# V spread over the partitions by TensorE, a smaller first load of constants, one more half of gate rows on TensorE, and a re-planned order, in a one-core mLSTM and mixer kernel

## The chip, the cores and the metric

One core of one Trainium2 chip. The metric is the device time of one execution in microseconds (us); the time before is given as a median of three runs, and one further execution was profiled.

## The reference

An mLSTM attention over B = 4 batches, 8 heads, 768 steps and head size 40, then a channel mixer on its output x (4 x 768 x 320).

```python
for t in range(S):
    m_new = np.maximum(f_gate[:, :, t] + m, i_gate[:, :, t])
    f_stab = np.exp(f_gate[:, :, t] + m - m_new); i_stab = np.exp(i_gate[:, :, t] - m_new)
    C = f_stab * C + i_stab * (v_t outer k_t);  n = f_stab * n + i_stab * k_t
    y[:, :, t] = sigmoid(o_t) * (C q_t) / max(|n q_t|, 1)
h = x^T @ U @ V            # U: 768 x 32, V: 32 x 768, along the sequence
u = x + h^T
out = u + relu(u @ w_ch1) @ w_ch2      # 320 -> 1280 -> 320
```

The weights U, V, w_ch1 and w_ch2 come as float64 bits and are turned into float32 on the chip.

## The kernel before

Each batch is cut into two halves of 384 steps, each half into six chunks of 64 steps. For every half, `half` inside `attention` loads q and k (`load_qk`), k and v by token (`load_tk`) and the output gate (`load_o`), makes the chunk states (`kv`, `state`), the scores, the decay weights (`decay_exp` or `decay_scan`, `weigh`), the numerator (`pv` and `inter`) and the normalized, gated result in the tile x. `rows` multiplies x with U, `mix` spreads the result with V (`vst`) and adds x (`cols`, the tile ut), and `mlp` does the two large products (`up` with w1, `down` with w2). Each operand of the large products is split into a high and a low part (`w_high`, `w_low`, `ut_high`, `ut_low`, `relu_high`, `relu_low`).

**Order.** Nothing is issued where it stands in the text. Each step is registered with `p.op(kind, priority, engine, cost, function, reads, writes, new tiles)`, and `Plan.schedule` simulates the engines with those costs and issues the steps in the order that it finds. Priorities are shifted by `ORDER`, `ORDER0` (batch 0) and, for one instance of a kind, by `MOVED`. Tiles of a kind share a few buffers (`SLOTS`): three of kind "fd" hold rows broadcast over partitions, five of kind "x" hold x and, at the start, gate data. PSUM has three banks of kind "m2" and five of kind "ps"; the kinds "st", "at" and "m1" share those five (`SHARE`). Transfers go out on SyncE's queue ("sp"), two at the start on ScalarE's ("aq"). When TensorE would be idle in the first part of the run, `keep_busy` puts in fillers: products of the tile zeros (`warm`, records `m<-zeros` or `ps<-zeros`). `Plan.words` keeps count of TensorE's instructions and, by an assumed page of 256 instructions, delays the plan where the next page would not have arrived; `PAGE, SENT_ON, FETCH` are its constants.

**V.** `keep_v` (L668) receives V as float32 in a tile of 128 partitions by 192 (`VN`). `store_v` writes it to the DRAM tensor vsd, two `load_v` (L681) read it back, each half of 384 columns repeated four times over 32 partitions, into an "fd" tile. `v_high` (ScalarE, L684) scales it with a column of the constants, `v_low` (L687) subtracts, and the result is vst, read by `cols` and by the first `down`.

**Constants.** `load_consts` (L507) loads 256 columns of cst_in into cst: the identity (128 columns), a mask and three columns of zeros and ones, `C_MP, C_MV, C_MU`, used as scales in `rows_high` (L1058), `v_high` and `ut2_high` (L1095).

**Gate rows.** q is multiplied with a cumulated decay g, which is needed repeated over 64 partitions for each head. `early[1]` decides, by `4 * hf + 8 * b < GB_FROM`, whether TensorE makes the repeated rows in PSUM (`two_rows`, records `ps<-gst,cst`, eight products per pair of heads) or SyncE loads them from DRAM (`rows_of("g", ...)`, records `fd<-gsd`). With `GB_FROM = 8` TensorE makes them for both halves of batch 0, and the two halves of batches 1, 2 and 3 load them. `q_decay` (L926) multiplies.

Products and weight loads of TensorE all have line L411 (the helper `mm`), transfers line L414 (`send`).

Of the kernel before, what the change touches and what calls it, by code (L numbers as in the profile page):

```python
# [19 lines left out]
RANK = 32  # L20
# [27 lines left out]
FB_FROM, GB_FROM = 12, 8  # L48
# [5 lines left out]
ALT_PRI = 1679.3  # L54
# [9 lines left out]
    "sigmoid": -38.7, "cols": -41.6,  # L64
# [5 lines left out]
AHEAD, IN_FLIGHT, SEEN, FLIGHT_TO = 1600.0, 970000.0, 150.0, 70000.0  # L70
# [34 lines left out]
STAY, TO_QUARTERS, FROM_QUARTERS = -32.2, 120.0, 180.0  # L105
WORDS = {"scores": 96, "pv": 48, "logs": 24, "log_turn": 96, "g": 16, "up": 8, "down": 6, "cols": 8, "rows": 4, "gate_turn": 48, "totals": 16}
TABLE = {"gate_exp": 1, "gate_input_exp": 1, "decay_exp": 1, "sigmoid": 2}
TABLE_LOAD, TABLE_STAY = 1283.0, 763.5
MARGIN, PLAIN = 37.5, {"up", "down"}
MOVED = {  # L110
    "again": {7: -414},
    "cols": {8: 345, 15: 1025},
    "down": {3: 37, 15: 37, 24: 2, 25: 2, 26: 37, 28: 37, 34: 37, 36: 37, 38: 37, 48: 2, 49: 2, 50: 37, 54: 37, 60: 505, 61: 460,
# [4 lines left out]
    "gate_shift": {0: 105},  # L118
    "kv": {4: 20, 6: 1282, 7: -579},
    "load_decay": {0: 453, 2: -485, 3: -22},  # L120
    "load_g": {2: 73, 13: 319, 19: 42, 20: 86, 21: 62},
    "load_gates0": {0: -1168},
    "load_o": {1: 29, 2: -829, 3: 75, 4: 255, 5: -389, 6: 386, 8: 532, 11: 132},
    "load_qk": {0: -1226, 1: -1267, 2: -779, 3: -1534, 4: -1058, 5: -1000, 6: -664, 7: -558, 13: -1338, 16: 191, 22: 223,
        24: 246, 26: 69, 30: 805},
    "load_tk": {0: -705, 1: -501, 2: -190, 3: -273, 4: 94, 6: 291, 8: 323},
    "load_v": {0: -364, 1: -515},
    "load_weights": {0: 63, 10: 73, 11: 81},
    "norm": {3: 120},
    "out_norm": {2: -130, 3: -492, 9: -257},  # L130
    "pv": {7: 435, 10: 221, 24: 375, 27: -186, 28: 469},
    "q_decay": {25: 305},
    "rows": {1: 261, 2: 418, 8: 132, 13: 541, 15: 777, 17: 387, 18: 124},
    "scores": {3: -1036, 10: 444, 12: 232},
    "state": {12: -92, 14: 159, 16: 220, 27: 461},
    "state0": {7: -386},
    "store_decay": {0: -1444, 1: 276},
    "store_g": {0: -284, 1: 149},
    "store_v": {0: 229},
    "u_low": {0: -343},  # L140
    "up": {16: 36, 32: 36, 40: 424, 43: 116, 44: 424, 46: 424, 58: 424, 64: 507, 78: 215, 81: 61, 82: 61, 83: 243, 84: 243,
        96: 61, 104: 61},
    "upto": {0: 250},
    "ut_high": {8: 356, 10: -148},
    "v2": {8: -907},
    "v_high": {0: -226},
    "vi": {0: 675, 8: 376, 10: -769, 11: -122, 15: -181},
    "w13_high": {2: 909},
    "w13_low": {3: 273},
    "w_high": {5: 70},  # L150
    "w_low": {2: -269},
    "weigh": {24: 475},
    "weight_rebase": {19: 381},
    "weight_shift": {13: 486},
    "weight_tail": {5: 409, 11: -509},
    "x_low": {0: -449, 2: 247, 17: -670},
# [3 lines left out]
PAGE, SENT_ON, FETCH = 256, 64, 2900.0  # L160
# [3 lines left out]
class Plan:  # L164


    def __init__(self, slots):
        self.kind_of, self.count, self.spare = [], [], []
        self.slots = {tag: [[tile, 0.0, None, tag] for tile in tiles] for tag, tiles in slots.items()}
        self.ops, self.at, self.busy, self.port = [], {}, defaultdict(float), []  # L170
        self.writer, self.readers = {}, defaultdict(list)
        self.batch = 0
        self.fetched, self.page_at = 12, {}
        self.seen = Counter()
        self.placed_by, self.uses, self.slot, self.held = {}, Counter(), {}, Counter()
# [40 lines left out]
    def words(self, n, at, cost, dma):  # L216

        a, late = self.fetched, 0.0
        self.fetched += n
        for x in range(a, self.fetched + 1):  # L220
            if x > a and (x + SENT_ON) % PAGE == 0:
                t = at + late + cost * (x - a) / n
                page = (x + SENT_ON) // PAGE
                self.page_at[page + 1] = max(t + max(0.0, dma - t), self.page_at.get(page, 0.0)) + FETCH
            if x < self.fetched and x % PAGE == 0:
                late += max(0.0, self.page_at.get(x // PAGE, 0.0) - (at + late + cost * (x - a) / n))
        return late
# [160 lines left out]
def mlstm_mixer_kernel(  # L388
# [43 lines left out]
    cst = const.tile([P, C_HSEL], F32, name="cst")  # L432
    ident = cst[:, C_IDENT:C_IDENT + P]
# [16 lines left out]
    vsd = dram.tile([RANK, S], F32, name="vsd")  # L450
# [38 lines left out]
    def gates():  # L489
# [17 lines left out]
        p.op("load_consts", -97, "aq", dma(P * C_HSEL * 4), lambda: send(nc.scalar, out=cst, in_=cst_in[:, 0:C_HSEL]), w=[("cst",)])  # L507
# [160 lines left out]
    def keep_v(pri, kc, t):  # L668

        p.op("store_v", pri, "sp", dma(P * VN * 4), lambda: send(nc.sync, out=vsd.rearrange("r (a n) -> (r a) n", n=VN), in_=t()), r=[kc], w=[("vsd",)])  # L670
        for c in range(2):
            cs = slice(c * HS, (c + 1) * HS)
            k4, kv = ("v4", c), ("vm", c)

            def v4(k4=k4):
                return T[k4][:, 0:HS]

            def load(cs=cs, v4=v4):
                send(nc.sync, out=v4(), in_=vsd[:, cs].unsqueeze(0).to_broadcast([P // RANK, RANK, HS]))
# [56 lines left out]
    def attention(b, base):  # L736
# [10 lines left out]
        def half(hf, n):  # L747
# [40 lines left out]
            for e2 in range(2):  # L788
                p.op("v2", at(n - 1), ("pool", "dve"), (pool(VO) * 0.79, dve(VO)), lambda e, e2=e2: e.tensor_mul(  # L789
                    v2flat()[:, e2], vflat()[:, e2], tokv(1, hf)[:, e2]),  # L790
                     r=[(kt, "v", 0), (kt, "v", 1), ("tok", hf, 1)], w=[(kv2, e2)], new=[(kv2, "v2")] if e2 == 0 else [])
            for e2 in range(2):
                p.op("vi", at(n - 1), ("pool", "dve"), (pool(VO) * 0.79, dve(VO)), lambda e, e2=e2: e.tensor_mul(  # L793
                    vflat()[:, e2], vflat()[:, e2], tokv(0, hf)[:, e2]),
                     r=[("tok", hf, 0), (kt, "v", 0), (kt, "v", 1), (kv2, e2)], w=[(kt, "vi", e2)])
# [10 lines left out]
            def chunks():  # L806
                def kvmm():
                    for j in range(nk):
# [8 lines left out]
                     w=kk, new=[(k, "at") for k in kk], stream="att", load=0.85, words=32 * nk)  # L817
# [226 lines left out]
        for c in range(NC):  # L1044
# [13 lines left out]
            lambda: nc.scalar.activation(T[kr], T[kp][:, 0:DM], AF.Copy, scale=cst[:, C_MP:C_MP + 1]),  # L1058
            r=[kp, ("cst",)], w=[kr], new=[(kr, "prr")],
# [4 lines left out]
    def mix(b, hf, pri):  # L1064
# [4 lines left out]
        for c in range(3):  # L1069
# [30 lines left out]
    def mlp(b, hf, pri):  # L1100
# [32 lines left out]
        def down(m, n):  # L1133
# [16 lines left out]
            p.op("down", pri + m + LAG + 0.5, "pe", 588 if m == 0 else 441, ops, r=r, w=[ka], new=[(ka, "m2")] if m == 0 else [])  # L1150
# [134 lines left out]
```

## Time and profile before

| what | us |
|---|---|
| median of three runs | 352.3 (350.09 to 355.05) |
| the profiled execution, its own time | 350.27 |
| its span, first to last instruction | 348.5 |
| TensorE busy in the span | 333.6 |
| VectorE, ScalarE, GpSimd busy | 209.7, 120.9, 68.0 |

The times of the engines are sums of recorded spans. TensorE's busy time holds the fillers, too. A record that ends in brackets, `[1.11 <-issue]`, tells how long its engine was idle before it and what ended that; "issue" is a wait for nothing that the profile shows. PE is TensorE, DVE VectorE, ACT ScalarE, POOL GpSimd, SPq the queue of SyncE.

### The profile page before, as it was taken

What the parts mean: (1) busy time and instruction counts of PE and PEld (TensorE: products, weight loads), DVE (VectorE), ACT (ScalarE), POOL (GpSimd) and SP (SyncE); (2) the same over time, 40 slices, a digit from 0 to 9 for tenths busy, and PEclk for the clock granted to TensorE, in tenths of its full rate; (3) what the DMA queues carried; (4) which work ended last, traced back from release to release, by engine and by line L of the source; (5) the groups of instructions that cost most, each with busy time, mean ns of one, the idle gap of its engine ahead of it and who ended that gap; (6) DMA issues with size and microseconds to landing.
All of it is one profiled execution on the core that took longest, in us unless ns stands there. A gap on an engine that the chain in (4) does not pass through costs nothing.

```text
span 348.5 us, 11236 instructions
## 1 busy us (share of the span) xinstructions
PE 333.6 (96%) x4794; PEld 305.5 (88%) x4794; DVE 209.7 (60%) x457; ACT 120.9 (35%) x279; POOL 68.0 (20%) x83
## 2 busy tenths in 40 slices
PE   8987898999999999989999999899999999999996
PEld 5655665799999999989899998799999999999996
DVE  7799897878985657965873229771575133121322
ACT  5258377646732034123143124210434122011220
POOL 1232524323260101422041006260030000000000
PEclk9999998999999999999999999989999999999999
DMA  6879656779845492575574103430010000100101
GB/s 180 186 220 229 187 175 194 223 218 256 241 134 197 136 222 81 182 176 130 150 192 132 44 2 93 156 86 2 3 58 3 0 2 0 56 2 0 58 0 56
DMA packets 23002, 40.63 MB, mean 117 GB/s; under 512 B 4201, under 2 KB 15721, under 8 KB 22953
## 3 DMA queue, kind: packets, MB, share of 16 engines
q1 hardware_dynamic: 22760, 39.70, 40.8%
q8 instruction: 37, 0.61, 0.7%
q10 hardware_dynamic: 192, 0.23, 0.2%
q14 instruction: 13, 0.10, 0.1%
HBM read 35.68 MB, written 4.23 MB: 115 GB/s over the span
## 4 chain that ended last, share of the span: by engine, by line
PE 77%; DMA 10%; DVE 4%; SPq 4%; issue 4%; ACT 1%; DVEq 0%; ACTq 0%
PE ps L411 46%; PE m L411 31%; SPq L414 4%; DMA kv<-in_tk 4%; DMA fd<-gsd 2%; DMA raw<-in_w 2%; DMA qk<-in_qk 2%; DVE dm L935 1%; DVE qd L926 1%; DVE cv L649 1%; DVE cv L651 0%; DVE x L1015 0%; DVE kv L793 0%; DVE wt L943 0%; ACT h L1049 0%
## 5 line engine op out<-in xcount | busy, mean ns | idle before, releaser
L411 PE MATMUL m<-w2h,h 128*128 128x320 f32 x480 | 119.6, 314 | 0.0
L411 PE MATMUL ps<-ut,w1h 128*128 128x384 f32 x400 | 117.3, 343 | 0.5 <-DVE wt L943 0.2
L1130 DVE SCALAR_TENSOR_TENSOR h<-ps,h 128x384 fp32r<-128x384 f32 x80 | 43.1, 553 | 77.0 <-ACT h L1128 69.2
L411 PEld LDWEIGHTS m<-w2h,h 128*128 128x128 f32 x480 | 83.4, 188 | 1.3 <-DVE h L1130 0.3
L1128 ACT ACTIVATE h<-ps 128x384 fp32r<-128x384 f32 x80 | 38.4, 490 | 126.6 <-PE m L411 86.3
L411 PE MATMUL ps<-ut,w1l 128*128 128x384 f32 x240 | 81.2, 338 | 0.0
L411 PEld LDWEIGHTS ps<-ut,w1h 128*128 128x128 f32 x400 | 74.4, 190 | 2.2 <-DVE wt L943 0.5
L411 PE MATMUL m<-w2l,h 128*128 128x320 f32 x240 | 74.3, 310 | 0.0
L411 PEld LDWEIGHTS ps<-ut,w1l 128*128 128x128 f32 x240 | 45.6, 190 | 0.0
L411 PEld LDWEIGHTS m<-w2l,h 128*128 128x128 f32 x240 | 45.3, 189 | 0.1
L1010 POOL TENSOR_TENSOR og<-og,rd 128x480 f32<-128x480 f32 x13 | 13.4, 1037 | 64.1 <-DVE rd L1005 57.9
L935 DVE TENSOR_TENSOR_SCAN dm<-fd,ident 128x384 f32<-128x384 f32 x20 | 21.2, 1070 | 3.9 <-DMA fd<-fsd 3.9
L411 PE MATMUL ps<-qk 40*64 40x64 f32 x768 | 17.3, 223 | 4.5 <-issue 3.0
L411 PEld LDWEIGHTS ps<-qk 40*64 40x64 f32 x768 | 14.6, 134 | 7.7 <-issue 4.7
L1153 DVE TENSOR_TENSOR o<-m,x 128x320 f32<-128x320 f32 x24 | 11.0, 486 | 14.5 <-PE m L411 14.4
L943 DVE TENSOR_TENSOR wt<-ps,dm 128x384 f32<-128x384 f32 x32 | 16.3, 548 | 4.8 <-PE ps L411 4.8
L411 PEld LDWEIGHTS <-zeros 128*128 128x128 bf16 (+1 forms) x114 | 10.7, 104 | 7.8 <-issue 4.9
L789 POOL TENSOR_TENSOR v<-kv,tok 128x492 f32<-128x492 f32 x7 | 9.0, 1292 | 37.3 <-PE ps L411 27.2
L411 PE MATMUL m<-zeros 128*128 128x256 bf16 x104 | 15.5, 287 | 0.1
L411 PE MATMUL ps<-cst,x 128*128 128x128 f32 (+2 forms) x168 | 15.1, 237 | 0.0
L926 DVE TENSOR_TENSOR qd<-qk,fd 104x320 f32<-104x320 f32 (+1 forms) x18 | 9.3, 519 | 9.0 <-DMA fd<-gsd 8.6
L830 POOL TENSOR_TENSOR Ct<-C,dect 104x164 f32<-104x164 f32 x16 | 9.3, 582 | 27.3 <-DVE C L831 27.1
(113 smaller groups left out, 410.4 us busy)
## 6 DMA issues: line engine op xcount, KB each, us to landing
kv<-in_tk SPq DMA_DIRECT2D x16, 486.0 KB
qk<-in_qk SPq DMA_DIRECT2D x64, 120.0 KB
raw<-in_w SPq DMA_DIRECT2D x20, 320.0 KB
og<-in_tk SPq DMA_DIRECT2D x16, 240.0 KB
fd<-fsd SPq DMA_DIRECT2D x40, 96.0 KB
out<-o SPq DMA_DIRECT2D x24, 160.0 KB
fd<-gsd SPq DMA_DIRECT2D x24, 96.0 KB
fd<-gsd SPq DMA_DIRECT2D x24, 80.0 KB
```

Of the source, the lines that this page charges most:

```text
L411: nc.tensor.matmul(o, a, b, start=start, stop=stop, **kw)
L414: p.sent = queue.dma_start(**kw).ins
L649: p.op("weight_shift", pri, "dve", 69 + n / 1.92, lambda tu=tu: V.tensor_scalar(tu(), tu(), 3, None, ALU.logical_shift_left), w=[kc], port ...
L789: p.op("v2", at(n - 1), ("pool", "dve"), (pool(VO) * 0.79, dve(VO)), lambda e, e2=e2: e.tensor_mul(v2flat()[:, e2], vflat()[:, e2], tokv(1 ...
L830: e.tensor_mul(t, cview(hf, j - 1)[r], dect[r, hf, b, :, j:j + 1].to_broadcast([Q + D, NP, DV]))
L926: e.tensor_mul(T[kqd][:, tg], T[kqk][:, 0, tg], T[kgb][0:Q + D, tg])
L935: lambda: nc.vector.tensor_tensor_scan(T[kdm], T[kfb][:, 0:HS], ident6, 0.0, ALU.mult, ALU.add),
L943: p.op("weigh", at(u), "dve", dve(HS), lambda: nc.vector.tensor_mul(T[kw], T[ks][:, 0:HS], T[kdm]), r=[ks, kdm], w=[kw], new=[(kw, "wt")])
L1010: p.op("out_norm", pf, ("pool", "dve"), (pool(KO) * 0.79, 900), lambda e, m=m, rdv=rdv: e.tensor_mul(otv(m), otv(m), rdv().unsqueeze(3).to ...
L1128: p.op("relu_high", pri + m - 1000, "act", 371, lambda: nc.scalar.activation(T[kh][:, 0, :], T[kp][:, 0:HS], AF.Relu), r=[kp], w=[(kh, 0)] ...
L1130: p.op("relu_low", pri + m - 1000, "dve", dve(HS), lambda: nc.vector.scalar_tensor_tensor(T[kh][:, 1, :], T[kp][:, 0:HS], 0.0, f32(T[kh][: ...
L1153: p.op("residual", pri - 1000, "dve", dve(DM), lambda: nc.vector.tensor_add(T[ko], T[ka][:, 0:DM], T[X][:, n, 0:DM]), r=[ka] + [(X, m) for ...
```

## The change

V is no longer sent through DRAM. ScalarE builds a selection matrix out of the identity (`v_pick`, 512 elements), in a tile of kind "x", and four products of 192 columns (`v_rows`, two for each half) write the repeated V into PSUM tiles of kind "st"; `v_high` and `v_low` read it there, and `v_low` is VectorE's alone. The first load of constants is cut to the identity (128 columns), and a small transfer on SyncE, `load_cols`, brings the columns of scales. `GB_FROM` goes from 8 to 12: the first half of batch 1 gets its gate rows from TensorE. The plan's page model, its constants and its counts of instructions are changed, and so are the priorities. `v2` and `vi` are only written differently.

```diff
-FB_FROM, GB_FROM = 12, 8
+FB_FROM, GB_FROM = 12, 12
-ALT_PRI = 1679.3
+ALT_PRI = 1765.5
-    "sigmoid": -38.7, "cols": -41.6,
+    "sigmoid": -38.7, "cols": -120.0,
-AHEAD, IN_FLIGHT, SEEN, FLIGHT_TO = 1600.0, 970000.0, 150.0, 70000.0
+AHEAD, IN_FLIGHT, SEEN, FLIGHT_TO = 1500.0, 1070000.0, 150.0, 70000.0
-STAY, TO_QUARTERS, FROM_QUARTERS = -32.2, 120.0, 180.0
+STAY, TO_QUARTERS, FROM_QUARTERS = -197.1, 120.0, 180.0
-TABLE_LOAD, TABLE_STAY = 1283.0, 763.5
-MARGIN, PLAIN = 37.5, {"up", "down"}
+TABLE_LOAD, TABLE_STAY = 1283.0, 1078.0
+MARGIN, PLAIN = 0.0, {"up", "down"}
 MOVED = {
...
-PAGE, SENT_ON, FETCH = 256, 64, 2900.0
+PAGE, SENT_ON, FETCH = 256, 64, 2750.0
...
-        self.fetched, self.page_at = 12, {}
+        self.fetched, self.page_at = 18, {}
...
-        for x in range(a, self.fetched + 1):
-            if x > a and (x + SENT_ON) % PAGE == 0:
-                t = at + late + cost * (x - a) / n
-                page = (x + SENT_ON) // PAGE
-                self.page_at[page + 1] = max(t + max(0.0, dma - t), self.page_at.get(page, 0.0)) + FETCH
-            if x < self.fetched and x % PAGE == 0:
-                late += max(0.0, self.page_at.get(x // PAGE, 0.0) - (at + late + cost * (x - a) / n))
+        for x in range(a, self.fetched):
+            if (x + SENT_ON) % PAGE == 0:
+                page, t = (x + SENT_ON) // PAGE, at + late + cost * (x - a) / n
+                wait = max(0.0, self.page_at.get(page, 0.0) - t)
+                late, t = late + wait, t + wait
+                self.page_at[page + 1] = max(t, dma, self.page_at.get(page, 0.0)) + FETCH
...
-    cst = const.tile([P, C_HSEL], F32, name="cst")
-    ident = cst[:, C_IDENT:C_IDENT + P]
+    ident = const.tile([P, P], F32, name="ident")
+    groups = const.tile([P, 3], F32, name="groups")
...
-        p.op("load_consts", -97, "aq", dma(P * C_HSEL * 4), lambda: send(nc.scalar, out=cst, in_=cst_in[:, 0:C_HSEL]), w=[("cst",)])
+        p.op("load_consts", -97, "aq", dma(P * P * 4), lambda: send(nc.scalar, out=ident, in_=cst_in[:, 0:P]), w=[("cst",)])
+        p.op("load_cols", 0, "sp", dma(P * 12 * 4), lambda: send(nc.sync, out=groups, in_=cst_in[:, C_MP:C_MU + 1]), w=[("cols",)])
...
     def keep_v(pri, kc, t):
-        p.op("store_v", pri, "sp", dma(P * VN * 4), lambda: send(nc.sync, out=vsd.rearrange("r (a n) -> (r a) n", n=VN), in_=t()), r=[kc], w=[("vsd",)])
+        kpick, reps = ("pick",), P // RANK
+        def pick():
+            return T[kpick].rearrange("p c d -> p (c d)")[:, 0:reps * P].rearrange("p (a x) -> p a x", x=P)
+        p.op("v_pick", pri - 1, "act", 50 + act(reps * P), lambda: nc.scalar.copy(
+            pick().rearrange("p a (n r) -> p a n r", n=reps),
+            ident.rearrange("p (r a) -> p a r", a=reps).unsqueeze(2).to_broadcast([P, reps, reps, RANK])), r=[("cst",)], w=[kpick], new=[(kpick, "x")])
         for c in range(2):
...
-            p.op("load_v", pri, "sp", dma(P * HS * 4), load, r=[("vsd",)], w=[k4], new=[(k4, "fd")], stream="v", load=0)
+            def spread(kp=kp, c=c):
+                for n in range(2):
+                    mm(T[kp][:, n * VN:(n + 1) * VN], pick()[:, 2 * c + n], t(), skip_group_check=True)
+            p.op("v_rows", pri, "pe", 2 * 4 * VN / 2.4 + 60, spread, r=[kc, kpick], w=[kp], new=[(kp, "st")], stream="mix", words=8)
...
-            p.op("v_low", pri, *both(HS), lambda e, kv=kv, v4=v4, cs=cs: e.tensor_sub(
-                vst[:, cs], v4(), f32(T[kv])), r=[k4, kv], w=[("vst", c)])
+            p.op("v_low", pri, "dve", dve(HS), lambda kv=kv, kp=kp, cs=cs: nc.vector.tensor_sub(
+                vst[:, cs], T[kp][:, 0:HS], f32(T[kv])), r=[kp, kv], w=[("vst", c)])
```

## Rows read from the trace of the kernel before

**Rows 1.** The page: TensorE's busy time, and its granted clock in 40 slices.

```profile
PE 333.6 (96%) x4794; PEld 305.5 (88%) x4794; DVE 209.7 (60%) x457; ACT 120.9 (35%) x279; POOL 68.0 (20%) x83
...
PEclk9999998999999999999999999989999999999999
```

**Rows 2.** Busy time by stretch: length, PE, PEld, DVE, ACT, POOL, clock, DMA share, GB/s.

```profile
0.00:65.00 65.00, 56.82 (x1411) 38.95 (x1411) 55.28 (x133) 39.53 (x85) 21.17 (x29) 0.97 0.72 195
65.00:130.00 65.00, 64.48 (x752) 60.63 (x753) 50.13 (x111) 27.49 (x69) 16.42 (x17) 1.00 0.73 204
130.00:240.00 110.00, 106.97 (x1752) 101.81 (x1752) 69.03 (x141) 29.11 (x73) 27.70 (x35) 0.98 0.41 115
240.00:348.50 108.50, 105.29 (x884) 104.11 (x882) 35.29 (x73) 24.74 (x54) 2.71 (x3) 1.00 0.05 19
...
28.00:65.00 37.00, 31.06 (x817) 21.83 (x810) 32.01 (x82) 26.02 (x57) 14.91 (x18) 0.95 0.68 192
```

**Rows 3.** The same for instructions on the tile zeros, the fillers (PE first).

```profile
0.00:65.00 65.00, 18.54 (x114) 10.66 (x114) 0.17 (x1) 1.25 (x1) 0.97 0.72 195
...
28.00:65.00 37.00, 7.01 (x50) 4.23 (x50) 0.00 (x0) 0.00 (x0) 0.95 0.68 192
```

**Rows 4.** PE's waits: sum, times, longest; two before 66 us, the last behind.

```profile
PE ps L411 <- issue: 2.7, 3, 1.0
PE ps L411 <- DMA qk<-in_qk: 1.1, 1, 1.1
...
PE ps L411 <- issue: 2.8, 3, 1.4
```

**Rows 5.** Timeline of PE: start, us, record; two of seven waits for issue.

```profile
29.27 0.49 PE L411 MATMUL m<-C,qd 40*64 40x41 f32 x19 [1.11 <-issue]
...
225.54 0.40 PE L411 MATMUL ps<-qk 40*64 40x64 f32 x11 [1.38 <-issue]
```

**Rows 6.** Timeline of PE: first large product in, first behind the second clock drop.

```profile
227.98 0.52 PE L411 MATMUL ps<-ut,w1h 128*128 128x384 f32 x1
...
230.71 0.33 PE L411 MATMUL ps<-ut,w1l 128*128 128x384 f32 x1
```

**Rows 7.** Timeline, 53 to 62 us: V's loads, its split, and its first reader.

```profile
53.01 1.26 SPq L414 DMA_DIRECT2D fd<-vsd  x2
...
58.75 0.62 ACT L684 ACTIVATE rru<-fd,cst 128x384 fp32r<-128x384 f32 x1 [1.17 <-DMA fd<-vsd]
...
60.38 0.62 DVE L1042 TENSOR_TENSOR pst<-ps,prr 128x320 fp32r<-128x320 f32 x2 [0.43 <-ACT prr L1058]
...
61.21 0.62 ACT L684 ACTIVATE rru<-fd,cst 128x384 fp32r<-128x384 f32 x1 [0.86 <-DMA fd<-vsd]
...
61.37 0.42 PE L411 MATMUL ps<-vst,pst 128*128 128x384 f32 x1
```

**Rows 8.** The chain that ended last, before 65 us: start, us, what.

```profile
51.50 3.23 DMA qk<-in_qk
...
54.80 7.09 DMA raw<-in_w
```

**Rows 9.** Timeline of SPq: first and last of four pairs of gate-row loads.

```profile
37.79 1.13 SPq L414 DMA_DIRECT2D fd<-gsd  x2
...
61.95 1.50 SPq L414 DMA_DIRECT2D fd<-gsd  x2
```

**Rows 10.** Timeline: the nearest rows to the added products and the added copy.

```profile
20.00 0.75 PE L411 MATMUL ps<-gst,cst 64*64 64x320 f32 x8
...
34.94 0.67 ACT L661 CAST u<-cv 128x576 fp32r<-128x576 f32 x1
...
46.06 0.81 PE L411 MATMUL ps<-x,u 128*128 128x320 f32 x2
```

**Rows 11.** Timeline of PE: a wait for the product of q and g.

```profile
64.05 0.78 PE L411 MATMUL ps<-C,qd 40*64 40x41 f32 x36 [0.68 <-DVE qd L926]
```

**Rows 12.** Timeline of ACT: the first reader of the constants.

```profile
4.01 1.03 ACT L554 COPY ident<-cst 64x384 f32<-64x384 f32 x2 [0.26 <-DMA cst<-in_cst_in]
```

More of the change, by code (lines that the diff above doesn't have):

```diff
@@ L104 @@
 QUARTERS = {"logs", "log_turn", "g", "scores", "kv", "pv", "inter", "gate_turn", "totals"}
-STAY, TO_QUARTERS, FROM_QUARTERS = -32.2, 120.0, 180.0
-WORDS = {"scores": 96, "pv": 48, "logs": 24, "log_turn": 96, "g": 16, "up": 8, "down": 6, "cols": 8, "rows": 4, "gate_turn": 48, "totals": 16}
+STAY, TO_QUARTERS, FROM_QUARTERS = -197.1, 120.0, 180.0
+WORDS = {"scores": 98, "pv": 48, "logs": 24, "log_turn": 98, "g": 16, "up": 8, "down": 6, "cols": 8, "rows": 4, "gate_turn": 48, "totals": 16}
 TABLE = {"gate_exp": 1, "gate_input_exp": 1, "decay_exp": 1, "sigmoid": 2}
-TABLE_LOAD, TABLE_STAY = 1283.0, 763.5
@@ L109 @@
-MARGIN, PLAIN = 37.5, {"up", "down"}
+TABLE_LOAD, TABLE_STAY = 1283.0, 1078.0
+MARGIN, PLAIN = 0.0, {"up", "down"}
 MOVED = {
-    "again": {7: -414},
-    "cols": {8: 345, 15: 1025},
-    "down": {3: 37, 15: 37, 24: 2, 25: 2, 26: 37, 28: 37, 34: 37, 36: 37, 38: 37, 48: 2, 49: 2, 50: 37, 54: 37, 60: 505, 61: 460,
[4 rows of a table removed]
[L118 to L156, printed above, removed]
@@ new lines @@
+    "again": {3: 561},
+    "cols": {6: 194, 8: 558, 11: -508, 15: 592},
+    "down": {4: -17, 5: -17, 7: -17, 8: -17, 15: 59, 26: 59, 28: 59, 29: -17, 32: 22, 36: 59, 49: -17, 50: 59, 54: 59, 61: 251,
[4 rows of a table added]
+    "fence": {2: -495, 3: -2310},
+    "gate": {1: -206},
+    "gate_shift": {0: 410},
+    "gate_w": {0: 1196},
+    "idents": {0: 221},
+    "inter": {6: -814, 8: -824, 11: -762},
+    "kv": {1: 795, 4: 300, 5: 342, 6: 1486},
+    "load_cols": {0: 109},
+    "load_decay": {0: 725, 1: 257, 2: 558, 26: 349, 27: 1265},
@@ new lines @@
+    "load_gates0": {0: -304},
+    "load_o": {0: 234, 1: -398, 6: 553, 8: 763},
+    "load_qk": {8: 208, 12: -173, 15: 329, 16: 505, 21: 326, 22: 389, 30: 1058},
+    "load_tk": {0: 96, 2: 192, 5: 412, 6: 658, 7: 31},
+    "load_weights": {0: 239, 1: 330, 3: -521, 4: 125, 9: 50, 10: -311, 12: -1221, 13: 251},
+    "out_norm": {7: -781},
+    "pv": {13: 676, 15: -760, 17: -864, 19: -610, 23: -252, 24: 575, 26: 834, 28: 1094},
+    "q_decay": {13: 295},
+    "residual": {15: 1582},
+    "rows": {9: 52, 15: 483, 16: 169},
@@ L157 @@
+    "rows_low2": {0: 1972},
+    "scores": {12: -404, 15: -647},
+    "spread": {0: -1577},
+    "state": {11: 234, 13: -385, 14: -406, 16: 195, 21: 422},
+    "store_decay": {0: 265, 1: 479},
+    "store_g": {0: 196, 1: 533},
[8 rows of a table added]
+    "w_high": {0: -316, 4: 140},
+    "w_low": {2: -434, 13: 157},
+    "weigh": {7: -415},
+    "weight_rebase": {5: -397, 9: -1504},
+    "weight_shift": {8: 243, 10: 543},
+    "weight_tail": {0: 338, 4: -438, 5: -509, 11: -670, 13: -215},
+    "x_high": {1: -804},
 }
@@ L668, in keep_v @@
     def keep_v(pri, kc, t):
-        p.op("store_v", pri, "sp", dma(P * VN * 4), lambda: send(nc.sync, out=vsd.rearrange("r (a n) -> (r a) n", n=VN), in_=t()), r=[kc], w=[("vsd",)])
+        kpick, reps = ("pick",), P // RANK
[4 more added lines that the diff above has]
+            ident.rearrange("p (r a) -> p a r", a=reps).unsqueeze(2).to_broadcast([P, reps, reps, RANK])), r=[("cst",)], w=[kpick], new=[(kpick, "x")])
         for c in range(2):
             cs = slice(c * HS, (c + 1) * HS)
[L673 to L679, printed above, removed]
-            p.op("load_v", pri, "sp", dma(P * HS * 4), load, r=[("vsd",)], w=[k4], new=[(k4, "fd")], stream="v", load=0)
+            kp, kv = ("v4", c), ("vm", c)
+            def spread(kp=kp, c=c):
+                for n in range(2):
+                    mm(T[kp][:, n * VN:(n + 1) * VN], pick()[:, 2 * c + n], t(), skip_group_check=True)
+            p.op("v_rows", pri, "pe", 2 * 4 * VN / 2.4 + 60, spread, r=[kc, kpick], w=[kp], new=[(kp, "st")], stream="mix", words=8)
             p.op(
                 "v_high", pri, "act", 120 + act(HS),
-                lambda kv=kv, v4=v4: nc.scalar.activation(T[kv], v4(), AF.Copy, scale=cst[:, C_MV:C_MV + 1]),
-                r=[k4, ("cst",)], w=[kv], new=[(kv, "rru")],
-            )
-            p.op("v_low", pri, *both(HS), lambda e, kv=kv, v4=v4, cs=cs: e.tensor_sub(
-                vst[:, cs], v4(), f32(T[kv])), r=[k4, kv], w=[("vst", c)])
+                lambda kv=kv, kp=kp: nc.scalar.activation(T[kv], T[kp][:, 0:HS], AF.Copy, scale=groups[:, 1:2]),
+                r=[kp, ("cols",)], w=[kv], new=[(kv, "rru")],
+            )
+            p.op("v_low", pri, "dve", dve(HS), lambda kv=kv, kp=kp, cs=cs: nc.vector.tensor_sub(
+                vst[:, cs], T[kp][:, 0:HS], f32(T[kv])), r=[kp, kv], w=[("vst", c)])
     def keep_hl(name, wh, wl, c, fs, rows):
@@ L787, in half @@
                 p.op("load_o", at(n + 4) - 8, "sp", dma(P * KO * 4), load_o, w=[(ko, m)], new=[(ko, "og")] if m == 0 else [])
[L788 to L795, printed above, removed]
+            for name, n2, dst in (("v2", 1, v2flat), ("vi", 0, vflat)):
+                for e2 in range(2):
+                    p.op(name, at(n - 1), ("pool", "dve"), (pool(VO) * 0.79, dve(VO)), lambda e, e2=e2, n2=n2, dst=dst: e.tensor_mul(
+                        dst()[:, e2], vflat()[:, e2], tokv(n2, hf)[:, e2]),
+                         r=[("tok", hf, n2), (kt, "v", 0), (kt, "v", 1)] + ([(kv2, e2)] if n2 == 0 else []),
+                         w=[(kv2, e2) if n2 else (kt, "vi", e2)], new=[(kv2, "v2")] if n2 and e2 == 0 else [])
             for m in range(2):
@@ L816, in chunks @@
                 p.op("kv", at(n - 0.5), "pe", 50 + 148 * nk, kvmm, r=[(kt, "k", 0), (kt, "k", 1), (kv2, 0), (kv2, 1)],
-                     w=kk, new=[(k, "at") for k in kk], stream="att", load=0.85, words=32 * nk)
+                     w=kk, new=[(k, "at") for k in kk], stream="att", load=0.85, words=32 * nk + 1)
                 r = slice(0, Q + D)
@@ L1057, in attention @@
             "rows_high", base + RP, "act", 50 + act(DM),
-            lambda: nc.scalar.activation(T[kr], T[kp][:, 0:DM], AF.Copy, scale=cst[:, C_MP:C_MP + 1]),
-            r=[kp, ("cst",)], w=[kr], new=[(kr, "prr")],
+            lambda: nc.scalar.activation(T[kr], T[kp][:, 0:DM], AF.Copy, scale=groups[:, 0:1]),
+            r=[kp, ("cols",)], w=[kr], new=[(kr, "prr")],
         )
@@ L1095, in mix @@
                 p.op("ut2_high", pri - 200, "act", 464, lambda kp=kp, kr=kr: nc.scalar.activation(
-                    T[kr], T[kp][:, 0:HS], AF.Copy, scale=cst[:, C_MU:C_MU + 1]), r=[kp, ("cst",)], w=[kr])
+                    T[kr], T[kp][:, 0:HS], AF.Copy, scale=groups[:, 2:3]), r=[kp, ("cols",)], w=[kr])
                 p.op("ut2_low", pri - 200, "dve", dve(HS), lambda kp=kp, kr=kr: nc.vector.tensor_sub(
@@ L1149, in down @@
                 r += [(kst, 0)] + [("vst", c) for c in range(2)]
-            p.op("down", pri + m + LAG + 0.5, "pe", 588 if m == 0 else 441, ops, r=r, w=[ka], new=[(ka, "m2")] if m == 0 else [])
+            p.op("down", pri + m + LAG + 0.5, "pe", 588 if m == 0 else 441, ops, words=8 if m == 0 else 6, r=r, w=[ka], new=[(ka, "m2")] if m == 0 else [])
             if last:
```

1 line of the change is left out of this document (removed), and 16 rows, old and new, of the table MOVED.

## The prediction

> **What bounds the kernel now.** I read the page first: TensorE is busy 333.6 of 348.5 us [rows 1], so the question is what the remaining 14.9 us are, and how much of the busy time is no work. The table by stretches cuts the run in two [rows 2]. Up to 65 us TensorE is busy 56.8 us, and the same table for the tile zeros gives 18.5 us of that to fillers [rows 3]: 38.3 us of work in 65, so 26.7 us are lost. From 65 us on it is busy 64.5 + 107.0 + 105.3 = 276.7 of 283.5 us, with no fillers. Of the 6.8 us missing there, 2.8 us are waits for "issue" [rows 4]; the stretch from 240 us lacks 3.2 us, nearly all behind the last product. So behind 65 us an engine other than TensorE hardly matters: the end comes when TensorE has worked off its list. Time can be gained in three ways: the front gets shorter (the large products start sooner, or more attention of batch 1 is done among the fillers), the waits for "issue" go, or the stretches of half clock go.
>
> What holds the front is in the chain that ended last: from 51.5 to 61.9 us it is two transfers, q and k with 3.23 us and weights with 7.09 us [rows 8], and TensorE waited 1.1 us itself for q and k [rows 4]. From 28 to 65 us the DMA share is 0.68 at 192 GB/s, and VectorE is busy 32.0 of 37 us [rows 2], so neither is quite full. The "issue" waits are seven: 2.7 us in three and one of 1.11 before 66 us, 2.8 us in three behind, 6.6 us together [rows 4, 5]. They stand inside runs of many small products (both rows shown cut one such run in two), where instructions are used up fastest; that fits instructions arriving late, but the profile names no cause. [...]
>
> **The change part by part.** The sum is made against the profiled execution: 350.27 us, its span of 348.5 and 1.8 around it. The median, 352.3, lies 2.0 above.
>
> *V.* One store and two loads go from SyncE's queue, and with them the wait of ScalarE: 1.17 and 0.86 us idle in front of the two scalings [rows 7]. V is not late for its first reader: the first half is scaled by 59.4 us, while the other operand, pst, is ready at 60.38 + 0.62 = 61.0, and the reader starts at 61.37. What goes is a detour of ScalarE right before the first large products: the second scaling occupies it until 61.8, and behind it in its queue stand a weight conversion and the copies of ut that the large products need. Bounds: 0 (the weights that arrive at 61.9 are awaited anyway) and 0.86 + 0.62 = 1.5 us. I take 0.7 gained, the middle, as the chain passes through both. Added are a copy of 512 elements on ScalarE, about 0.67 x 512/576 = 0.6 us, and four products of 192 columns: two of 320 took 0.81 us, so 0.81/2 x 192/320 = 0.24 each, 1.0 together [rows 10]. U's weights, that arrived just before V's, were split at 35 us [rows 10], so these steps can run then, when TensorE still has 7.0 us of fillers to 65 us [rows 3]; I cost them at nothing, and at +1.0 if they run where no filler is left. The four steps of the split stay and move earlier.
>
> *Gate rows of batch 1, first half.* Eight loads of 80 KB leave SyncE's queue, four pairs of 1.1 to 1.5 us between 38 and 63 us [rows 9]. TensorE gets two groups of eight products; one such group took 0.75 us [rows 10], so 1.5 us. Fillers cover it again, 2.5 of 7.0 us with V; without that cover it costs +1.5. The products with q stay.
>
> *The transfers.* 8 x 80 KB of gate rows, 96 + 2 x 192 KB of V and 64 KB of constants are 1.2 MB less, at 192 GB/s 6.3 us of traffic. That is one end; the other is 0, if what is freed was hidden. The wait of TensorE nearest to it is the 1.1 us for q and k, issued right behind two of the loads and the store that go; the weights behind them come sooner too. I take 1.5 gained, near that row, and keep 0 and 6.3 for the range.
>
> *The first constants.* Their first reader waited 0.26 us for them [rows 12]; VectorE's chain of gates, which runs beside it, did not. Bounds 0 and 0.26 gained; I take 0. The transfer added on SyncE is one issue of some 0.4 us among transfers that nobody waits for yet: 0.
>
> *The page model and the priorities.* They issue nothing, they only reorder. Bounds: all seven waits gone, 6.6 us gained, and as many again behind 65 us, 2.8 lost. Runs of small products remain and have to be fetched, so most waits should stay; I take 1.5 gained, one wait in the front and part of one behind. The half clock follows such waits: the second drop covers 2.7 us of large products [rows 6], at half speed 1.4 us lost. I take half of one such drop, 0.7 gained, with bounds of 2.8 gained (both drops) and 2.8 lost (two more). The new priorities alone I take at 0, between 2 lost and 2 gained, for no row prices them.
>
> [...]
>
> Sum: 0.7 + 1.5 + 1.5 + 0.7 = 4.4 us gained, 345.9 for an execution like the profiled one, and 2.0 more, 347.9, on the scale of the median.
>
> **The rivals.** (a) Hidden: the front is held by VectorE (busy 0.87 of it, [rows 2]) and the order of its queue, the transfers were covered, and the waits for "issue" only move. What is left is V's 0.7 us, nearly nothing else: 351.5. For it speaks that the chain runs through VectorE's queue from 62 us to the first large product; against it, that two transfers fill the ten us before.
>
> (b) The front was paced by transfers. Then most of the 6.3 us comes back, with two or three waits for "issue" and the clock drop that follows the wait at 54: 5 + 2.5 + 1.4 = 8.9 us gained, 343.4. For it: V's loads, issued at 53.0, were used at 58.75 and 61.21 and lay beside the weights' 7.09 us [rows 7, 8]. Against it: a DMA share of 0.68 [rows 2]. [...]
>
> (c) Slower: PSUM. The added g rows need two of the five shared banks at once, beside scores and decay rows of the same half, and free them only after VectorE's product with q, for which TensorE already once waited 0.68 us [rows 11]. If the two groups are pushed behind 65 us, no filler pays for them: 1.5 + 1.0 of products, two such waits of 0.7, and a new half-clock stretch of 1.4 are 5.3 lost, less 1.5 of transfers, 3.8 lost: 356.1. It decides from the point at which the groups run later than the first large product.
>
> **How the numbers follow.** What three runs can tell is about 2%, 7 us: below 345.3 or above 359.3. Forecast 0.50, (a) 0.25, (b) 0.16, (c) 0.09. The likeliest gives 347.9, its own range 345 to 350.5. To hold 8 in 10 the range takes in (a) and all but the far end of (b), and leaves out most of (c): 343.0 to 353.0. Faster by over 2%: most of (b), 0.13, and the low edge of the forecast, 0.06, so 0.19; slower by over 2%: the far part of (c), 0.04; within: 0.77.
>
> **What would show it.** V right: no transfer on vsd, four products from V's tile near 35 to 45 us, vst written before 50 us. Transfers right: TensorE's wait for q and k near 54 us gone, and the first product of ut with w1 before 63.5 us (now 64.9). Gate rows right: fillers from 28 to 65 us down to about 4 us with no more real work lost. Page model right: the sum of "issue" waits of TensorE at 4 to 5 us. The prediction is wrong if the first large product starts later than now, if "issue" waits grow, or if TensorE waits for VectorE's products with q.

## The result, and the profile after

The changed kernel takes 347.56 us (median of 20 executions, 343.89 to 352.3), the kernel before 352.65 (20, 347.65 to 357.25). The ratio is 0.9876, 95% interval [0.9843, 0.9909]: 4.4 us less, as much as the sum of the prediction, and under the 2% that count as faster. Every ratio here leaves out the executions that took over 1.5% longer than the fastest of their kernel, so this one is not the quotient of the two medians, which are 5.1 us apart. The profiled execution took 347.63 us, with a span of 345.9; against the profile of before it is 2.6 us shorter, so the pair shows somewhat less than the medians.

TensorE's busy time and its granted clock on the page of the changed kernel:

```profile
PE 332.8 (96%) x4799; PEld 307.1 (89%) x4799; DVE 208.9 (60%) x462; ACT 121.2 (35%) x280; POOL 61.5 (18%) x78
...
PEclk9989789999999999999999999999999999999999
```

The slice near 230 us that stood at 8 before [rows 1] stands at 9; the lower slices now lie in the front alone. The table by stretches, with the columns of [rows 2]:

```profile
28.00:65.00 37.00, 31.50 (x791) 22.87 (x784) 29.18 (x77) 21.34 (x49) 11.84 (x14) 0.91 0.73 197
0.00:65.00 65.00, 56.64 (x1409) 41.35 (x1410) 53.46 (x133) 36.17 (x80) 16.93 (x25) 0.92 0.73 196
65.00:130.00 65.00, 64.50 (x758) 61.38 (x757) 51.06 (x113) 30.80 (x75) 16.80 (x18) 1.00 0.64 180
130.00:240.00 110.00, 109.13 (x1774) 103.16 (x1773) 69.71 (x145) 30.62 (x76) 25.78 (x33) 1.00 0.41 117
240.00:346.00 106.00, 102.55 (x864) 101.17 (x862) 34.62 (x72) 23.56 (x51) 1.99 (x3) 1.00 0.06 20
```

From 65 us to the end there are now 280.9 us instead of 283.5; so the whole difference of the two spans lies behind 65 us. TensorE is idle there for 4.7 us (0.50 + 0.87 + 3.35) where it was 6.8, and busy 0.6 us less. Nearly all of the idle time that went is in the stretch from 130 to 240 us, which lost 3.0 us before and loses 0.9 now. The front looks the same in sum: 56.64 us busy instead of 56.82. Its inside is different. The fillers, the same table for the tile zeros:

```profile
0.00:65.00 65.00, 16.09 (x95) 0.92 0.73 196
28.00:65.00 37.00, 4.80 (x29) 0.91 0.73 197
```

So 2.45 us of fillers [rows 3] went, and their place was taken by products of V and gate rows and by a lower clock (0.92 instead of 0.97). TensorE's waits, before 66 us and then behind (sum, times, longest):

```profile
PE ps L411 <- issue: 3.4, 3, 1.7
PE m L411 <- issue: 2.2, 2, 2.0
...
PE ps L411 <- DVE x L1018: 0.7, 1, 0.7
...
PE m L411 <- DVE h L1133: 0.6, 1, 0.6
PE ps L411 <- DVE h L1133: 0.4, 1, 0.4
PE ps L411 <- issue: 0.2, 1, 0.2
```

The wait for q and k [rows 4] is gone. The waits for "issue" fell from 2.8 to 0.2 us behind 66 us and grew from 3.8 to 5.6 in the front. The chain that ended last still passes a transfer of weights in the front, 6.40 us where there were 3.23 and 7.09 [rows 8]:

```profile
52.38 3.62 PE ps L411 x62
...
58.49 6.40 DMA raw<-in_w
```

And the timeline shows the new steps, and the first large product:

```profile
3.79 1.12 ACT L675 COPY x<-ident 128x512 f32<-128x512 f32 x1
...
41.48 2.93 PE L411 MATMUL ps<-cv,x 128*128 128x192 f32 x8
...
43.78 0.56 DVE L692 TENSOR_TENSOR vst<-ps,rru 128x384 fp32r<-128x384 f32 x1
48.83 0.49 DVE L692 TENSOR_TENSOR vst<-ps,rru 128x384 fp32r<-128x384 f32 x1
53.65 0.77 PE L411 MATMUL ps<-gst,ident 64*64 64x320 f32 x8
61.78 0.77 PE L411 MATMUL ps<-gst,ident 64*64 64x320 f32 x8
66.86 0.44 PE L411 MATMUL ps<-ut,w1h 128*128 128x384 f32 x1
```

### The profile page after: what moved, and what is told of

Same layout as the page of the kernel before. It is cut to its first block, busy times and chain, and to the rows that moved or that the text cites. A ratio compares the mean times of both kernels' runs of the same rounds, so it can differ in the third digit from the quotient of the medians.

```text
span 345.9 us, 11218 instructions
## 1 busy us (share of the span) xinstructions
PE 332.8 (96%) x4799; PEld 307.1 (89%) x4799; DVE 208.9 (60%) x462; ACT 121.2 (35%) x280; POOL 61.5 (18%) x78
## 4 chain that ended last, share of the span: by engine, by line
PE 89%; DMA 4%; issue 3%; DVE 2%; SPq 0%; ACT 0%; POOL 0%; DVEq 0%; POOLq 0%; ACTq 0%
PE ps L411 52%; PE m L411 37%; DMA fd<-gsd 2%; DMA raw<-in_w 2%; SPq L414 0%; DVE x L1018 0%; DVE h L1133 0%; ACT C L825 0%; POOL qd L929 0%; DVE wt L946 0%; DVE cv L651 0%; DVE qd L929 0%; DVE o L1156 0%; DVE Ct L833 0%; DVE rd L1010 0%
## 5 line engine op out<-in xcount | busy, mean ns | idle before, releaser
L411 PEld LDWEIGHTS ps<-ut,w1h 128*128 128x128 f32 x400 | 73.4, 188 | 1.4 <-DVE ut L1100 0.3
L1013 POOL TENSOR_TENSOR og<-og,rd 128x480 f32<-128x480 f32 x12 | 12.1, 1016 | 34.5 <-DVE rd L1008 34.5
L411 PE MATMUL ps<-qk 40*64 40x64 f32 x768 | 15.8, 221 | 1.9 <-issue 1.5
L411 PEld LDWEIGHTS ps<-qk 40*64 40x64 f32 x768 | 13.7, 134 | 4.3 <-issue 2.2
L411 PE MATMUL ps<-ident,x 128*128 128x128 f32 (+2 forms) x168 | 15.2, 236 | 0.2 <-issue 0.2
L411 PEld LDWEIGHTS ps<-kv,wt 64*64 64x64 f32 x576 | 10.5, 134 | 4.9 <-issue 1.8
L833 POOL TENSOR_TENSOR Ct<-C,dect 104x164 f32<-104x164 f32 x13 | 8.2, 629 | 37.3 <-DVE C L834 25.1
L795 POOL TENSOR_TENSOR kv<-kv,tok 128x492 f32<-128x492 f32 x9 | 9.6, 1075 | 27.2 <-DVE v L795 27.1
L411 PEld LDWEIGHTS <-zeros 128*128 128x128 bf16 (+1 forms) x95 | 8.9, 106 | 6.0 <-issue 3.3
L411 PE MATMUL m<-zeros 128*128 128x256 bf16 x90 | 13.8, 290 | 0.0
```

The source lines that it names most:

```text
L411: nc.tensor.matmul(o, a, b, start=start, stop=stop, **kw)
L795: p.op(name, at(n - 1), ("pool", "dve"), (pool(VO) * 0.79, dve(VO)), lambda e, e2=e2, n2=n2, dst=dst: e.tensor_mul(dst()[:, e2], vflat()[: ...
L833: e.tensor_mul(t, cview(hf, j - 1)[r], dect[r, hf, b, :, j:j + 1].to_broadcast([Q + D, NP, DV]))
L1013: p.op("out_norm", pf, ("pool", "dve"), (pool(KO) * 0.79, 900), lambda e, m=m, rdv=rdv: e.tensor_mul(otv(m), otv(m), rdv().unsqueeze(3).to ...
```

## The experiments

Two theories stood after this reading. **L**: the gain is in the late waits for "issue", which the re-planned order avoids; V and the gate rows only change the front, where nothing came out shorter. **F**: V and the gate rows pay, because the front then leaves less work to be done behind it. "Late" waits are those behind 66 us.

To try parts without a new plan, the order that the plan had found was written into each kernel as a list, one step to a line (`kind number engine buffers`; `~` is a filler, with the number of pieces it is cut into; `>` says which transfer waits for which), and only the lines named below were changed. Line numbers in their profiles differ for that.

**e1: the changed kernel with its instructions shifted.** The first 48 fillers are cut in two. They take the same columns, and everything behind them stands 96 instructions later in TensorE's program.

```diff
-~ m2 0 1
+~ m2 0 2
...
```

> Order of the changed kernel, kept word for word; only the first 48 fillers are each cut into two halves of 128 columns, so that every later TensorE instruction stands 96 places further on against the pages of 256 instructions. Theory L (the gain is that behind 65 us no page ends inside a run of small products): TensorE's waits for issue behind 65 us go from 0.2 us to between 2 and 3.5 us, perhaps with a stretch of half clock, and the time goes back towards that of the kernel before: ratio to before 0.994 to 1.002. Theory F (the gain is V off DRAM, fewer transfers and the gate rows, in the front): ratio stays near 0.988, between 0.985 and 0.991.

Measured: 0.9906 [0.9865, 0.9947], TensorE's waits behind 66 us:

```profile
PE m L1975 <- DVE h L2697: 1.6, 1, 1.6
PE ps L1975 <- issue: 1.5, 2, 0.8
```

The waits for "issue" came back to 1.5 us, less than L wanted: where instructions stand in the program matters for them. The ratio lies in F's range, at its upper end; beside the changed kernel's 0.9876, and its 0.9893 in e8, the intervals overlap, so it is not shown that part of the gain went with them.

**e2: V and gate rows alone, in the old order.** As many records of fillers were taken out as products put in, so that the later instructions keep their numbers.

```diff
-FB_FROM, GB_FROM = 12, 8
+FB_FROM, GB_FROM = 12, 12
-load_g 0 sp fd.2
...
-load_g 7 sp 
+g 4 pe m2.1,m2.2
+g 5 pe ps.1,m2.0
-store_v 0 sp 
-load_v 0 sp fd.0
-load_v 1 sp fd.1
+load_cols 0 sp 
+v_pick 0 act x.0
+v_rows 0 pe ps.4
+v_rows 1 pe m2.1
...
```

> Order of the kernel before, kept word for word, with the two parts of the change that move work: V by four products on TensorE with the small load of constants, and the gate rows of batch 1, first half, on TensorE. Each added product takes the place of as many instructions of fillers, so that pages end where they ended. Theory L: waits for issue behind 65 us stay at 2.8 us within 0.5, ratio 0.996 to 1.003. Theory F: the whole gain or most of it, ratio 0.986 to 0.992, and the first large product at or before 63.5 us.

Measured: a median of 351.62 us (344.16 to 356.42, 6) beside 354.36 of before, too few for an interval. The profile had 3.0 us of late waits for "issue", and its first large product started at 66.17 us, not by 63.5 as F wanted. The kernel was run again as e7 and e10.

**e3: five steps moved, nothing else.** Late in the old order, five steps of large products are put into runs of small ones, so that instructions are used up more slowly there.

```diff
-down 63 pe 
...
+down 63 pe 
+up 47 pe 
...
-down 122 pe m2.0
...
+down 122 pe m2.0
+down 124 pe 
+down 125 pe 
...
```

> Kernel before, with five steps of the large products moved in the issue order and nothing else: one down step later and one up step earlier, both to stand in front of the kv step near 148 us, one down step later and two earlier, into the run of small products near 222 us. Theory L: the two long waits for issue there (1.12 and 1.38 us) and the half clock behind the second go; 2.5 to 4.2 us gained, ratio 0.988 to 0.993. Theory F: the waits are covered by other slack, ratio 0.998 to 1.002.

Measured: 0.9953 [0.9907, 0.9999], 1.7 us. Its waits behind 66 us:

```profile
PE ps L2008 <- DVE qd L2523: 1.7, 1, 1.7
PE ps L2008 <- issue: 0.6, 2, 0.4
```

2.2 us of "issue" went, and 1.7 us of the total, between the ranges of L and F. The wait of 1.7 us for q's product is the one of [rows 11], which falls behind 66 us in this execution, at 68.74. So L is right that the late waits cost time, though the interval ends just below 1, and the middle of it is less than half of the whole gain.

**e4: all three**, the edits of e2 and e3 together.

> Both edits together: V and the gate rows on TensorE in the old order, and the five moved steps. Theory L: as with the moved steps alone, within 1 us of it, ratio 0.986 to 0.994. Theory F: as with V and gate rows alone. If both parts pay, the gains add up.

Measured: 0.9822 [0.9757, 0.9888], late waits for "issue" 0.2 us. That is further than e3 (the intervals do not touch), so V and the gate rows pay something of their own, and pure L falls. What is V's and what the gate rows', the next four runs ask, on one chip.

**e5: V alone** (the V lines of e2's edit).

> V alone, everything else in the recorded order of before; the late runs of small products stay as they are, only shifted by V's 16 instructions. If the gain of the change is all in late waits for pages (theory L), the waits for issue behind 66 us stay at 2.5 to 3.2 us and the ratio is 0.997 to 1.003. If V's detour through DRAM cost what the prediction said (theory F), the ratio is 0.996 to 0.999 (0.7 us) and vst is written before 50 us without any gain behind 65 us. If the four products of V, run at half clock for 2.9 us, cost more than they free, it is 1.003 to 1.008.

Measured: 0.9972 [0.9934, 1.001]. Both theories' ranges hold this, so it doesn't part them. The late waits stayed (3.7 us), TensorE's wait for q and k is gone from the front, but the chain of the front shows what comes next when V's transfers are gone, the loads of gate rows:

```profile
43.55 4.87 DMA raw<-in_w
...
61.43 4.47 DMA fd<-gsd
```

**e6: the gate rows alone** (the lines of e2's edit with `GB_FROM`, `load_g` and `g`).

> Only the gate rows of batch 1's first half made by TensorE, in the recorded order of before; eight loads of 80 KB go, sixteen products of 0.1 us come. Theory L: ratio 0.997 to 1.003, late issue waits 2.5 to 3.2 us. Theory F (the transfers held the front): TensorE's wait for q and k near 54 us is gone and the ratio is 0.988 to 0.996 (1.5 to 4 us).

Measured: 0.993 [0.9875, 0.9985], in F's range, though the interval reaches into L's, with 3.2 us of late waits left, and the wait for q and k gone here as well. Now V's transfers are what the chain passes:

```profile
53.00 7.40 DMA fd<-vsd
```

**e7: V and gate rows again.**

> V and the gate rows together in the old order, for a ratio. Theory L: 0.997 to 1.003 with 3.0 us of late waits for issue. Theory F: 0.988 to 0.994, about the sum of the two parts, and with the five moved steps (0.9953 alone) 0.982 to 0.988, as was measured for all three. Of the executions, those at a mean granted clock of 0.995 or more should be 3 us shorter than those at 0.985, in both theories.

Measured: 0.9874 [0.9804, 0.9943], with late waits for "issue" as before the change:

```profile
PE ps L1968 <- issue: 3.3, 3, 1.6
PE ps L1968 <- DVE wt L2505: 0.2, 1, 0.2
```

Its chain passes no transfer between 41 and 70 us; VectorE's products and small products of TensorE stand there:

```profile
54.78 0.57 DVE x L2577
55.40 0.35 PE m L1968
55.99 0.87 PE ps L1968 x40
57.18 3.88 PE ps L1968 x30
61.09 0.54 ACT prr L2620
```

The gain is there with all late waits in place: F holds for these two parts together.

**e8: the changed kernel itself, beside them.**

> The changed kernel itself, on the same chip as its parts. Both theories: 0.984 to 0.991. If the order that the plan found adds something to V, the gate rows and the moved steps, it is below 0.982; if it gives back part of what they bring, it is above 0.985.

Measured: 0.9893 [0.9836, 0.995]. The late waits are 0.6 us, those of the front 7.0 (4.1 and 2.9), and the chain passes 4.11 us of weights at 50.20. So the new order adds nothing visible to V and the gate rows alone. Above 0.985 stood for an order that gives part back; the interval reaches below that, so it is not decided.

The next question was why the gate rows pay: because eight transfers of 80 KB leave the queues (**T**), or because nobody waits for what they bring, nor for their buffers (**B**).

**e9: the traffic put back.** e7 with the eight loads at their old places and with their old order among the transfers; they write a corner of w2l that is not yet in use, and nobody reads it.

```diff
+dummy_g 0 sp 
+> dummy_g 0 load_tk 5
+dummy_g 1 sp 
...
+> load_weights 13 dummy_g 7
```

> V and the gate rows on TensorE as before, but the eight loads of the gate rows stay at their places in SyncE's queue, with the order between transfers that hung on them; they write a corner of w2l that is not yet in use, and nobody reads what they bring. If the gate rows pay because eight transfers of 80 KB leave the front (theory T), 2 us of the gain go: ratio 0.992 to 0.998, and TensorE's waits in the front grow again by 1 to 2 us. If they pay because q's product no longer waits for the loads and their buffers (theory B), it stays at 0.985 to 0.990.

Measured: 0.9856 [0.9778, 0.9934]. From 28 to 65 us the transfers moved more than in e7, in the first line here e9, and no slower front followed:

```profile
28.00:65.00 37.00, 32.82 (x865) 22.27 (x857) 31.64 (x84) 26.93 (x59) 12.77 (x18) 0.93 0.71 201
```

(e7:)

```profile
28.00:65.00 37.00, 32.93 (x811) 22.18 (x805) 31.59 (x83) 27.54 (x61) 13.81 (x18) 0.93 0.63 181
```

The chain of e9 has no transfer between 41 and 70 us either. So 20 GB/s more cost nothing that can be seen, and the 2 us that T wanted are not there; a smaller price is not excluded, since the interval reaches to 0.9934. That leaves B, but no run tested B by itself, and the trace of before doesn't show its wait: VectorE was not idle before any of its four products of q with the loaded rows of this half (such records end without brackets). The last three:

```profile
56.67 0.48 DVE L926 TENSOR_TENSOR qd<-qk,fd 104x320 f32<-104x320 f32 x1
...
63.51 0.48 DVE L926 TENSOR_TENSOR qd<-qk,fd 104x320 f32<-104x320 f32 x1
...
65.94 0.48 DVE L926 TENSOR_TENSOR qd<-qk,fd 104x320 f32<-104x320 f32 x1
```

What the loads cost, through their buffers or through the transfers queued behind them, stays open.

**e10 and e11: V and gate rows, and all three, on that chip.**

> V and the gate rows without those loads, on the same chip: 0.985 to 0.990 in both theories, waits for issue behind 66 us at about 3 us.

> V, the gate rows and the five moved steps, in the old order. If the two gains add, 0.979 to 0.986, lower than V and the gate rows alone by 0.003 to 0.008, with waits for issue behind 66 us below 0.7 us; if the first such number was chance, 0.985 to 0.990.

Measured: e10 0.9932 [0.9867, 0.9997], late waits 3.9 us; e11 0.986 [0.9795, 0.9925], late waits 1.2, more than expected. Both stand higher than their first runs (e10 above its expected range, too), e11 below e10 by 0.007, as expected. In e10, the same kernel as e7, the chain does pass a transfer, of the output gate:

```profile
52.38 2.39 DMA og<-in_tk
```

All three in the old order gave 0.9822 and 0.986, the changed kernel 0.9876 and 0.9893: perhaps better by 2 us, but the intervals overlap, so no version here is shown to beat it.

**All runs at one clock.** Every execution lists its mean granted clock, and the spread of a kernel hangs on it: e2's one execution at 1.0 took 344.16 us, its four at 0.98 to 0.985 between 350.99 and 352.26. A fit over 178 executions, with a constant for each kernel (for before, one for each of the series e1 to e4, e5 to e8 and e9 to e11) and one slope, gives 1.4 us less (+- 0.2, as all errors here 95%) for each 0.005 more of mean clock, and against before at the same clock:

| | ratio as measured | us at the same clock |
|---|---|---|
| V (e5) | 0.9972 | -0.6 +- 1.3 |
| gate rows (e6) | 0.993 | -2.1 +- 1.3 |
| both (e2, e7, e10) | -, 0.9874, 0.9932 | -2.9, -2.8, -1.9 (+- 1.7 at most) |
| both, loads put back (e9) | 0.9856 | -2.5 +- 1.8 |
| five steps moved (e3) | 0.9953 | -2.5 +- 1.3 |
| all three (e4, e11) | 0.9822, 0.986 | -5.5, -5.0 (+- 1.7) |
| changed kernel (e8) | 0.9893 | -2.7 +- 1.7 |
| changed kernel shifted (e1) | 0.9906 | -1.5 +- 1.3 |

Within these errors the parts add up: 2.1 + 0.6 for both, and 2.5 more for the moved steps are 5.2. The loads put back in e9 cost 0.1 +- 1.8 us beside the mean of the three runs without them. The errors are on the small side: e1 to e4 and e5 to e8 ran on one chip, and the constants of before differ by 1.5 us between them. With one constant for that chip the rows of e1 to e4 become smaller, and those of e5 to e8 larger, by 0.7 us.

## Why the prediction came out right, point by point

**The sum.** 4.4 us were forecast and 4.4 measured. The four terms stood less well than their sum. That the two agree to a tenth is luck: the interval of the result alone goes from 3.2 to 5.5 us, and each term is known to 1.3 us at best.

**V: 0.7 us, measured 1.0** (0.0028 of 353.07, interval -0.4 to 2.3; 0.6 at the same clock). The detour through DRAM went as described, and vst was written by 44.3 and 49.3 us, before 50. Two prices were off. The first is the products: I read the two records of [rows 10] as two products, but they are one: V's four products stand as eight records, two for each, so each costs 0.46 us and not 0.24. In e5 the first two took 0.92 us at a granted clock of 1.00 (37.5 to 38.6 us), and in e7 either two did, 1.84 together. In the changed kernel the four took 2.93, with the granted clock at 0.50 from 41.4 to 44.5 us. The second is the copy `v_pick`, 1.12 us instead of 0.6. In e5 neither is seen to cost time: fillers went in their place, as forecast. In the changed kernel the chain passes V's products, 2.86 us from 41.55 us, so there their price at half clock isn't shown to be nothing. `v_pick` runs ahead of the first reader of the constants, which starts at 4.82 instead of 4.01 us [rows 12]; nothing in the runs shows a price for that, and it was not tried alone.

**Gate rows at nothing, transfers 1.5 us: 2.5 measured together** (e6, 0.007 of 353.07, interval 0.5 to 4.4). A group (four products, which leave eight records) took 0.77 us, forecast 0.75, and fillers paid for it: from 28 to 65 us they fell from 7.0 to 4.8, forecast about 4. The size was right, the reason half. I bounded the term by traffic, between 0 and 6.3 us at 192 GB/s, and e9 puts 640 of these 1184 KB back at no cost that is seen; V's loads and the constants were not put back. The value I took from a wait, TensorE's 1.1 us for q and k [rows 4], and that is gone in e9 too. But it is gone in e5 and in e6 as well, with gains of 1.0 and 2.5 us, so it doesn't price the term by itself. In the chains each part uncovers the other: without the gate rows' loads the chain falls to V's (7.40 us in e6), without V's to the gate rows' (4.47 us in e5). With both gone it passes no transfer from 41 to 70 us in e2, e7 and e9, and one of 2.39 us in e10. The times show no more than a sum: 0.6 and 2.1 us at the same clock for the parts, 1.9 to 2.9 for both.

**Page model 1.5, half clock 0.7.** This is what the pair of profiles shows as the whole gain: late waits from 2.8 to 0.2 us, and no half clock behind 65 us. e3 prices the first alone at 1.7 us, interval 0 to 3.3. The mean clock rose from 0.984 (62 executions of before, e1 to e11) to 0.990 (the 20 of the result) and 0.987 (e8); at 1.4 us for 0.005 that is 1.6 and 0.9 us, against 0.7. But e2, e7 and e10, one and the same kernel, have means of 0.985, 0.989 and 0.983, so a rise of this size is not shown to come from the change. The drop that I counted at half speed had a granted clock of 0.50, from 227.08 to 230.49 us, 1.5 us behind the end of the wait of 1.38; the other drop of before, 0.50 from 56.42 to 59.82 us, stands behind the wait for q and k, which ended at 54.77, and not behind one for "issue". That half clock follows such waits holds in part: of fourteen late waits of over 1 us, in seven profiles, five had a stretch of half clock beside or shortly behind them (one each in before, e2, e5, e7 and e10, whose mean clock from 130 to 240 us is 0.97 or 0.98, where the other eight have 1.00), and the six profiles without such a wait had none before the last products. One step failed: I took one wait of the front to go, and the sum of all to be 4 to 5 us. The front's grew from 3.8 to 5.6 us, the sum is 5.8, and in e8 it is 7.6, above the 6.6 of before: by that execution the second sign of being wrong ("if 'issue' waits grow") is met as well.

**The test that misled.** I wrote that the prediction is wrong if the first large product starts later than now. It starts at 66.86 instead of 64.92 us, and not before 63.5 as the forecast of the transfers had it, and the run is shorter. Up to there TensorE now has 1360 records of products that are no fillers (1455 records by the table, less 95), where it had 1296 (1410 less 114); V and the gate rows are 24 of the 64 more. The new order puts some 40 records of small products ahead of the large ones, so that start is no mark of the front's length. In the old order, too, it is later with V and the gate rows (65.57 to 66.73 us in e2, e7, e9 and e10), in a kernel that is faster.

**The rivals.** (a), hidden: wrong for the gate rows, by e6 and e7. (b), paced by transfers: it named the right rows, V's loads and the weights, but its 6.3 us did not come: the gate rows' share of the traffic cost nothing that is seen in e9, and V's share, which no run puts back, is by the fit no more than what both bring beyond e6, 0.4 +- 1.4 us. (c), PSUM: the second group ran at 61.78, ahead of the first large product, so its condition was not met; of its waits a trace remains, 0.7 us for VectorE's x, and in all seven runs that make these rows in the old order one of 1.5 to 1.8 us, in the middle of the first group.

**What stays open.** By the parts the changed kernel should stand near all three (-5.0 to -5.5 us), and it measures -2.7 +- 1.7 (with one constant for the chip, -3.5 beside -4.8 and -5.0). That may be chance. If not, the new order gives part back in the front: in both profiles of the changed kernel the chain passes weights again (6.40 and 4.11 us), and the waits for "issue" before 66 us are 5.6 and 7.0 us, where e2 has 0.4 and e7, e9 and e10 none. But neither mark decides: e4 has 4.3 us of such waits, and e11 a transfer of weights of 5.48 us in its chain. It was not tried by itself.

## What to carry to other kernels

When you take a transfer off the critical chain, ask which transfer the chain passes then: here each of two detours uncovered the other (7.40 us of V's loads in e6, 4.47 of the gate rows' in e5). The removed loads here were not worth their bytes over the rate of the queues: 640 KB at 192 GB/s are 3.4 us, and put back in e9 they cost 0.1 +- 1.8. Test such traffic by leaving the load in and the reader out. And when a change also re-plans the order, freeze the old order and put the parts into it one by one; profiles of two different orders don't tell whose gain it is.

## What the runs showed that was not expected

**The waits for "issue" have fixed places.** Counting TensorE's records in order (weight loads, products and semaphores), the waits of before stand at the numbers 1217, 1473, 1985, 2241, 5313, 6081 and 7617, those of the changed kernel at 705, 1217, 1473, 1729, 2753 and 4801, and each leaves 193 when divided by 256. The same holds of every such wait in the other eleven profiles, also in e1, where every step behind the first 48 fillers has a number 96 higher. The page counts 37 instruction packets of 0.61 MB together on queue q8 in either kernel, 16 KB each. So these waits hang on the number of an instruction and not on what it does, as they would if instructions arrived late in blocks of 256. The prediction had only found late instructions to fit, and no trace shows their arrival itself. Behind 66 us, in all thirteen profiles, a wait stands only where the last 256 records went by in less than 4.8 us, itself included, but not at every such place: before, they took 2.92 us at 149.92 and 3.57 at 225.54, with the two longest waits, and 3.42 at 222.0 with none. Where 256 records took 6 us or more, as among large products, the gap at the same place is at most 0.2 us.

**In the front the same places cost more**, up to 1.95 us in the changed kernel:

```profile
33.46 0.55 PE L411 MATMUL ps<-fd,after 64*64 64x384 f32 x4 [1.69 <-issue]
38.98 0.54 PE L411 MATMUL m<-kv,wt 64*64 64x41 f32 x10 [1.95 <-issue]
```

There 256 records took 5.5 to 5.9 us with the wait, and TensorE waited all the same, while the transfers moved 196 GB/s. That the instructions queue behind data there would fit, but e9 moved 201 GB/s from 28 to 65 us and had no such wait in the front, so the rate of the transfers alone doesn't make them. The cause stays open.
